# A gated mix of a long convolution and linear attention: the layout of three DRAM round trips, and the issue order of the second half

## The chip, the cores and the metric

The kernel runs on one core of a Trainium2 chip. The time is the device time of one execution in microseconds (us). Before the change it is 265.62 us, the median of 3 runs (265.59 to 265.95).

## The reference

The input `A_u` has 2048 rows of 512 columns (bf16). Two branches read it, and a gate per row mixes them:

```python
g = sigmoid((x * gate_w).sum(-1))
a = irfft(rfft(u) * rfft(K)) + u * Dskip      # K[d, l] = Re sum_n C exp(dt A l) dt B, 128 n per column d
phi_q = [softmax(q @ w_phi), softmax(-q @ w_phi)]    # 32 heads of 16; phi_k alike
o = phi_q (phi_k^T v) / (phi_q sum(phi_k) + 1e-6)
out = g * a + (1 - g) * (o @ wo)
```

The convolution runs along the 2048 rows, for each of the 512 columns.

## The kernel before, in words

**Steps and their order.** The kernel is a list of 1058 steps (class `Plan`). A step has an engine, a function that issues its instructions, and the steps on which it depends. Three strings written out by hand fix the rest: `ORDER` the order in which the steps are issued, `SIDES` which of two engines a movable step gets (mostly ACT or DVE), and `RINGS` which PSUM buffers it uses. Each engine executes its instructions in the order of issue. DMAs are issued on SP, except for a few stores of the result on ACT; a DMA that must wait for data holds up everything behind it on the engine that issues it. Steps that only mark the transfer or the arrival of a DMA issue nothing.

**Tables.** The convolution kernel K is made for 32 columns at a time, in sixteen tables 0 to 15. For each, DVE multiplies C and D tables into A (L1100, L1105, in half of the tables also a sum L1110), ACT makes E by exp and cs by sin, DVE makes a second E (L1053) and R from E and cs (L1117, L1121), and PE multiplies A and R (kps, L183). A has one buffer, R two. The result is cast to SBUF (KD), transformed by PE (psA, L190) and cast again (XA).

**Transforms.** The 512 columns are four groups of 128. Groups 0 to 2 are transformed whole, from four tables each; group 3 in three parts: tables 12 and 13 (64 columns), table 14 (32) and table 15 (32). A transform goes: PE psB (L196), cast XK, DVE multiplies by the spectrum XUX of the input, loaded from DRAM (t, L1231 or L1234), PE psz (L1263), cast Zr. Then the data must change partitions (the *turn*): Zr is stored in the DRAM scratch Zd (L1276) and loaded back as ZT (L1285). PE makes the output psy from ZT (L1341), and DVE scales it by the gate into xT (L1363, L1366). Table 15 goes without the turn: its psz (L1297) is cast to Z and used in SBUF (L1354, L1369). A group of 128 columns has four stores Zd and two loads ZT, one of each half of the partitions.

**Attention.** Blocks of 512 rows: pq, exp (Eq), the denominators zs, and a chain of small steps on ACT and DVE (z steps, L878 to L886) that gives the normaliser apm. It is stored to DRAM (apd, L899) and loaded back, each row copied to 16 partitions (ax, L906); DVE multiplies Eq by it (L913). Then follow the products ops (L932), their casts oT, and the output products bps (L946). Three blocks come early; the fourth, the *late* block, runs beside the last tables. Its bps are cast into xT (L981, L983), and stored by L995.

**Stores.** The result is stored by L1380 for groups 1 to 3 (group 1 together with group 0; of groups 0 to 2 the late block's rows are left to L995). Group 3 is stored in two sets: columns 384 to 447 when tables 12 and 13 are through, columns 448 to 511 at the end.

Of the kernel before, what the change touches and what calls it, by code (L numbers as in the profile page):

```python
# [70 lines left out]
class Plan:  # L71

    DIGITS = "0123456789abcdefghijklmnopqrstuvwxyzABCDEFGHIJKLMNOPQRSTUVWXYZ-_"
    ORDER = ("040B0H0K0d0y0C0D0L0s0I070J0M0P0g000S110j0N08010z0T0m0Q0e2R0a0p0q0r0_0W2T100U0O0V14120Y2U2x0A2S050k130Z2y2V2X2Z0R190v0t0u"
             "0b0c0w2_0l0E0X2W1516172L1a061b2Y022-30311y33340n030f0-"
             "0h1e1f0i1w2J18321c0F0o2B2K2M1n1z1H1g1A1o2D2C1d1p1I091x1E1J351Q1R2F1B0x1C2E0G2H1q36372G2I2P382N2Q391F3b2O3c4C1S3a4J4L4K4M"
             "3d3e4Q4R3f4U1Y3g4N1r4O1h4V3h1L4Y4-"
             "4P3i4Z4_3j4W4S53542z57504T3k4X1Z515b5d58521s1D593l5c3n5i5e55565j3m5a1G3o5q5f5g5s5r5t3p3r3q1T5m5n5u3s5v5h5o5k5w5x5B1P4D4E"
             "3w2v5l5p4F5y5F5C3y1U5H3x5G5I5J5z5A1V5D5E3t3z5U3D5K5V5M5N3A3R3E2w3F5W5L1O5_3G5O5Q5X5Y5Z3B3C1W605R5S1N3K3M1K3S1M5-"
             "5P3L634G642A615T653N673T6869626a666m6n6o3U6p3V3W3X3Y6b6c6q6d6r6s1t3Z3H3-1X3_3O1i1j41401_4221431-"  # L80
             "1k1l204445466e272923222b282d4748243P491m2a4a2c2e4b4g2f4c2g4d252h2o4e4h4i4n1u4j3u3v2j4p2i2l2k2m2q2p6i262s4q4o1v4k2n4u2r2t"
             "6f4v4w6j4r3I2u4x4y4z6g4l8l3J4A8p8m6t6u6k6v8q3Q4f4s6x6h8k8o6l8n8r8s6y6z6w6A6C4m4t4B8C6G8t6I6K8w8x8y8u6B6H6J4H8D8v6L6M6N7d"
             "8z8A8E4I8B7e7f8I7g8F6F9e8Q8G8H9b6O6P8R7h7j7i6Q6R8J9f7M7N8S6S6T6U6Vaeaf7O8W8X8K7k9g8L8T8U8Z8-"
             "938M8N7l6D8_7m8V7n6W6X6Y8O8P8Y7P94an7o7pao7q6_70717r90917Qa47S9295ag7R6Z7s6-"
             "72aha8a9966Ea7akaca5ai73aa75979998ajap7677a69aalatamab74ad7TaBaC7t797u7v7U78au7y7z7V7w7x9caq9naras7AavaH7W9d9h9o9paw7X9v"
             "aY9waK7Y7ZaDaL9q9raZ7a9x9y9zaIc57B7-aM9kc69D9EaQaEbX9L7Cb_aF7D9M7_9Ac07EaRaG9iaxaz80ay9B818285bYaA7Ga-"
             "7IaJ86879j9Fc19s7Jb-"
             "9l9m9Na_7bc7aNaOaPc3cbb2b37HbZc283aS9C7FaT849G9H9I9t89aUaWaV8baX7cccc8c99O9u9P9Q9R888cb87Kb9b0c4caceb19J8abacfcgbg8dck9K"
             "8ecl8f8gbbbh8hbcbibob4cP9Sbpbqcd9T8ichci7L8jcBcCcjcsdYcYctcucycDczdZd-cQcR9Ucmd_cHcvcw9W9Xcnbj9VbwbkblbxcocIbre0eLcp9Ze1"
             "e2b5b6eMbse3eUeVcxb7bye4cqbtbu9Ybdbe9-"  # L90
             "9_cAcrcSbme5cZdOdScEbfcFcGcTcUe6a0a1bve7dTdRdWeNa2e8cJcKe9bzbAedeecLeRcNcOa3eSeaebeOcMc_ePbBd0ecd1d7cVd8d9cWeCdfcXeWdPdU"
             "d2daefege-e_eQd3dbdQdgeTdVd4dndodXdhdcg1g2dieDeEdjeXbKfAbCbnbDbEbFeYfBeZf0f1bGc-dpbLddg7dqbHd5f2drbMf3f4f5bNfGbIbJbOezdk"
             "eAfDdsfEeBeIf6f7feffdldtbPdebQdBfCfHehdueifFejdmf8fgeJd6ekdvfIfJdyf9fafhfbg4fifKg5g6dwfjdzfkfcdxdCdEfLdAdFfMg3g8dGg9dHfN"
             "fleFelfdfmfpdDdLgagbgcgddIeGemeKfqeHfOfPfQfRgeenepfneofreqeresgfggghgifSfTfUfofsbRgjbSgkdJftetglfVfYfZgmgngobUbVgqfufWdM"
             "dNbWgpf-fvfxfygreufwevewexbTeydKfzfXf_g0gvgwgsgtgugx")
# [103 lines left out]
def prepare(P, nc, g, evict, psum):  # L199

    fc, act, persist, at = g.fc, g.act, g.persist, g.at
    F = Bag()
# [35 lines left out]
    S("ifc", lambda: nc.scalar.copy(out=F.fi[:], in_=F.ii[:]), r="ic0", w="ic1")  # L238
# [33 lines left out]
    def sine(out, v, kv, w, turn=False):  # L272
        S("tgs", lambda: act(out=out(), in_=(low(v()) if not turn else low(v()).rearrange("p (h t) -> p t h", h=2)), func=ACT.Sin, scale=TURN), r="act " + kv, w=w)
# [786 lines left out]
def plan_conv(P, nc, g, psum, r):  # L1060
# [130 lines left out]
    def transform(XA, ready, Q, off, nd, far, Ls, last, co=0, free=True, split=False):  # L1191
# [9 lines left out]
        if far:  # L1201
            F.Zd = g.dram.tile([32, 4, 32, nd], BF16, name=f"Zd{Q}_{off}")
# [423 lines left out]
```

## Time and profile before

| | |
|---|---|
| median of the runs | 265.62 us |
| the profiled execution | 266.07 us |
| its span, first to last instruction | 264.3 us |
| mean granted TensorE clock | 0.932 of full speed |
| busy: DVE, ACT, PE | 232.5, 221.5, 207.2 us |
| DMA packets | 63323, of which 40496 are under 512 B |
| last multiply of DVE ends | 257.69 us |

The profile is of one execution. A line L1231 is that line of the kernel; casts stand under the two lines of a helper (L149 on ACT, L151 on DVE), so they are told apart by their tiles. SPq and ACTq are the DMA issues of SP and ACT. The chain of work that ended last is followed back from the end, at each step to what released it; its pieces have a start, a length and a name.

### The profile page before, as it was taken

How to read it: one execution, taken by the hardware profiler on the slowest of the kernel's cores; microseconds unless marked ns; L12 is line 12 of the kernel's file. 1: busy time of each engine (PE TensorE's matmuls, PEld its weight loads, DVE VectorE, ACT ScalarE, POOL GpSimd, SP SyncE). 2: the span in 40 equal slices, each digit the busy share in tenths (PEclk: the TensorE clock that was granted, in tenths of full speed). 3: DMA queues.
4: the chain of work that ended last, by engine and by line, in shares of the span. 5: the costliest groups of instructions: out<-in, count | busy, mean ns of one | idle time of the engine just before them, and what ended most of it. 6: DMA issues, size and time to landing. Idle time of an engine off the chain costs nothing.

```text
span 264.3 us, 10050 instructions
## 1 busy us (share of the span) xinstructions
PE 207.2 (78%) x4491; PEld 143.7 (54%) x4512; DVE 232.5 (88%) x315; ACT 221.5 (84%) x305; POOL 8.2 (3%) x21
## 2 busy tenths in 40 slices
PE   0766999999864879889776768999997598999750
PEld 0655655656633533456555247665775176965540
DVE  6699989889799999999999997999997998997630
ACT  6999998998899999899999898999998597755100
POOL 4700000000000000000000000000000000000000
PEclk9999999999976599999998688999999799999985
DMA  6995000454501892204160655159554589999775
GB/s 201 189 219 171 0 4 2 122 145 138 154 8 36 245 266 97 82 20 153 56 195 9 208 195 167 42 162 180 142 172 147 172 203 234 188 189 162 156 110 96
DMA packets 63323, 35.93 MB, mean 136 GB/s; under 512 B 40496, under 2 KB 57776, under 8 KB 63280
## 3 DMA queue, kind: packets, MB, share of 16 engines
q1 hardware_dynamic: 61424, 34.76, 53.2%
q8 instruction: 35, 0.57, 1.0%
q10 hardware_dynamic: 1856, 0.52, 1.0%
q14 instruction: 8, 0.07, 0.1%
HBM read 22.17 MB, written 13.11 MB: 133 GB/s over the span
## 4 chain that ended last, share of the span: by engine, by line
DVE 35%; PE 34%; DMA 8%; issue 7%; ACT 7%; SPq 6%; DVEq 0%; ACTq 0%
PE pk L709 5%; PE vp L757 4%; DVE Eq L913 3%; DVE A L1105 3%; DVE A L1100 3%; DMA ZT<-Zd 3%; DVE R L1117 3%; DVE R L1121 3%; SPq L1492 3%; DMA ax<-apd 2%; PE kps L183 2%; DVE E L1053 2%; PE psz L1263 2%; PE kvp L774 2%; DMA apd<-apm 2%
## 5 line engine op out<-in xcount | busy, mean ns | idle before, releaser
L68 ACT ACTIVATE cs<-args 128x1024 bf16<-128x1024 f32 x32 | 30.7, 1067 | 0.7 <-PE args L1023 0.7
L183 PEld LDWEIGHTS <-A 128*32 128x32 bf16 x1536 | 26.5, 160 | 6.1 <-issue 2.3
L183 PE MATMUL kps<-R,A 128*32 128x64 bf16 x1536 | 28.2, 229 | 1.9 <-DVE R L1121 1.2
L1263 PE MATMUL psz<-t,TI 128*128 128x512 bf16 x51 | 17.4, 446 | 5.0 <-DVE t L1231 3.2
L1100 DVE TENSOR_TENSOR A<-Ctab,Dtab 128x2048 bf16<-128x2048 bf16 x16 | 19.5, 1216 | 1.6 <-PE kps L183 1.6
L149 ACT CAST Zr<-psz 128x1024 bf16<-128x1024 f32 x15 | 15.2, 1021 | 5.8 <-PE psz L1263 4.3
L1121 DVE TENSOR_TENSOR R<-E,cs 128x2048 bf16<-128x2048 bf16 x16 | 19.4, 1215 | 0.1
L1105 DVE TENSOR_TENSOR A<-Ctab,Dtab 128x2048 bf16<-128x2048 bf16 x16 | 19.4, 1216 | 0.0
L1117 DVE TENSOR_TENSOR R<-E,cs 128x2048 bf16<-128x2048 bf16 x16 | 19.4, 1215 | 0.0
L68 ACT ACTIVATE Ek<-pk 128x512 bf16<-128x512 f32 x32 | 16.7, 599 | 1.9 <-PE pk L709 1.7
L68 ACT ACTIVATE Eq<-pq 128x512 bf16<-128x512 f32 (+1 forms) x28 | 16.6, 685 | 0.8 <-PE pq L843 0.7
L1231 DVE TENSOR_TENSOR t<-XUX,XK 128x2048 bf16<-128x2048 bf16 x14 | 16.7, 1216 | 0.4 <-ACT XK L149 0.4
L68 ACT ACTIVATE E<-args 128x1024 bf16<-128x1024 f32 x16 | 16.4, 1035 | 0.5 <-DVE R L1121 0.5
L757 PE MATMUL vp<-WW,xT 128*128 128x512 bf16 x59 | 16.2, 406 | 0.7 <-issue 0.6
L149 ACT CAST XA<-psA 128x1024 bf16<-128x1024 f32 (+1 forms) x15 | 14.6, 1002 | 2.4 <-PE psA L190 2.4
L843 PE MATMUL pq<-xT,Wqp 128*128 128x512 bf16 x64 | 15.5, 380 | 0.3 <-ACT xT L149 0.3
L616 PE MATMUL psB<-XAu,TB 64*128 64x128 bf16 x256 | 11.6, 250 | 5.1 <-ACT xst L149 3.4
L149 ACT CAST XK<-psB 128x1024 bf16<-128x1024 f32 (+1 forms) x14 | 13.6, 989 | 2.2 <-DVE XK L151 1.3
L709 PE MATMUL pk<-WW,xT 128*128 128x512 bf16 x58 | 15.0, 380 | 0.4 <-issue 0.2
L616 PEld LDWEIGHTS <-TB 64*128 64x128 bf16 x256 | 9.6, 110 | 8.9 <-issue 8.8
L190 PE MATMUL psA<-W,KD 128*64 128x128 bf16 x256 | 10.0, 223 | 5.1 <-ACT cs L68 2.9
L65 ACT ACT_TABLE_LOAD x10 | 12.8, 1283 | 0.2
(211 smaller groups left out, 503.8 us busy)
## 6 DMA issues: line engine op xcount, KB each, us to landing
XUX<-XUd SPq DMA_DIRECT2D x32, 256.0 KB
XUd<-xst SPq DMA_DIRECT2D x8, 512.0 KB
ax<-apd SPq DMA_DIRECT2D x16, 256.0 KB
Zd<-Zr SPq DMA_DIRECT2D x15, 256.0 KB
ZT<-Zd SPq DMA_DIRECT2D x6, 512.0 KB
UD<-in_A_u_dram SPq DMA_DIRECT2D x16, 128.0 KB
XUd<-xst SPq DMA_DIRECT2D x8, 256.0 KB
wqk<-in_B_wqkv_dram SPq DMA_DIRECT2D x1, 1024.0 KB
```

What stands on the lines that cost most here:

```text
L68: return self.nc.scalar.activation(**kw)
L149: self.nc.scalar.copy(out=o, in_=i)
L183: nc.tensor.matmul(kps[32 * dj:32 * dj + 32, g4, e, :], lhsT=A[:, ka, :, :, d].rearrange("p a b -> p (a b)"), rhs=R[:, kr, d, :], start=(i ...
L616: nc.tensor.matmul(box.ps[:, c2, sl, :], lhsT=fc.TB[rows, b0:b0 + 2].rearrange("p a b -> p (a b)"), rhs=X.t[rows, k, r0 + sl].rearrange("p ...
L709: nc.tensor.matmul(box.ps[:], lhsT=xT[:, st, kt, :], rhs=g.WW[:, kt, :], start=(kt == 0), stop=(kt == 3))
L757: nc.tensor.matmul(box.ps[:], lhsT=xT[:, st, kt, :], rhs=g.WW[:, 4 + kt, :], start=(kt == 0), stop=(kt == 3))
L1100: nc.vector.tensor_tensor(out=c.A[:, 0:2].rearrange("p o a b c -> p (o a) b c"), in0=g.C[U // 8][:, 0:2, :, d0 % 256:d0 % 256 + 32].rearra ...
L1105: nc.vector.tensor_tensor(out=c.A[:, 2:4].rearrange("p o a b c -> p (o a) b c"), in0=g.C[U // 8][:, 1:3, :, d0 % 256:d0 % 256 + 32].rearra ...
L1117: nc.vector.tensor_tensor(out=c.R[:, :, :, 32:64], in0=t.E[:, 1].unsqueeze(1).to_broadcast([128, 2, 32, 32]), in1=t.cs[:], op=ALU.mult)
L1121: nc.vector.tensor_tensor(out=c.R[:, :, :, 0:32], in0=t.E[:, 0].unsqueeze(1).to_broadcast([128, 2, 32, 32]), in1=t.cs[:, ::-1, :, ::-1], o ...
L1231: nc.vector.tensor_tensor(out=box.t, in0=Ls[r0 // ns].X[:], in1=box.XK[:].unsqueeze(1).to_broadcast([128, 2, 1024]), op=ALU.mult)
L1263: nc.tensor.matmul(box.ps[:, hb, :], lhsT=fc.TI[:, k].rearrange("p t h a -> p (t h a)"), rhs=box.t[:, k, 512 * hb:512 * hb + 512], start=( ...
```

## The change

Six edits. The two tables of numbers are left out of the diff, but for a word.

1. The turn's scratch Zd is laid out by the row that loads it: row r holds all t and x of its columns in one run (8 KB for 128 columns), and rows are padded by 1024 elements. A store of Zr now writes pieces of 128 columns (256 bytes; 128 and 64 bytes in group 3), where it wrote 2 KB runs; a load ZT reads one run for each partition, where it read 32 pieces. Each load of half the partitions is issued as two of 32 partitions. The table TI gets its axes in the matching order.
2. The normaliser is stored twice (two DMAs apd), so that the load sees 16 rows of DRAM copied 8 times each, where it saw 8 rows copied 16 times.
3. Columns 384 to 511 are stored as one set at the end: four DMAs of 128 columns, where there were eight of 64 columns at two points. That leaves 1052 steps.
4. The very first cast (column indices to float) goes from ACT to DVE.
5. The steps from number 605 on are issued in another order. Up to DVE's multiply L913 of the third block, near 170 us in the trace, each engine has the rows that it had, apart from edits 2 and 4.
6. Of the movable steps behind that point some change engines. From DVE to ACT: an XK of group 1, an XA of group 2, the XK of table 14, half of XA, XK and Z of table 15, one cast of bps. From ACT to DVE: net one oT, the Zr of table 14, two scalings of bps (L983).

```diff
 class Plan:
-    ORDER = ("040B0H0K0d0y0C0D0L0s0I070J0M0P0g000S110j0N08010z0T0m0Q0e2R0a0p0q0r0_0W2T100U0O0V14120Y2U2x0A2S050k130Z2y2V2X2Z0R190v0t0u"
+    ORDER = ("0405060B0C0D0H0K0d0e0f0y0z0A0L0s0t0u0I0708090J0M0P0g0h0i000S110j0k0l0N0102030T0m0n0o0Q2R0a0b0c0p0q0r0_0W2T100U0O0V14120Y"
...
-    S("ifc", lambda: nc.scalar.copy(out=F.fi[:], in_=F.ii[:]), r="ic0", w="ic1")
+    V("ifc", lambda: nc.vector.tensor_copy(out=F.fi[:], in_=F.ii[:]), r="ic0", w="ic1")
...
         def aw():
-            nc.sync.dma_start(out=g.apd[b].rearrange("i h m c -> (i h m) c"), in_=Q.apm[:].rearrange("p s t -> p (s t)"))
+            for u in range(2):
+                nc.sync.dma_start(out=g.apd[b, :, :, u].rearrange("i h m c -> (i h) m c"), in_=Q.apm[:].rearrange("p s t -> p (s t)"))
...
-                                  in_=g.apd[b, i].rearrange("h m c -> h (m c)").unsqueeze(1).to_broadcast([8, 16, 1024]))
+                                  in_=g.apd[b, i].rearrange("h u m c -> (h u) (m c)").unsqueeze(1).to_broadcast([16, 8, 1024]))
...
-        lo = 64 if last else off
+        lo = 0 if last else off
...
-            F.Zd = g.dram.tile([32, 4, 32, nd], BF16, name=f"Zd{Q}_{off}")
+            F.Zd = g.dram.tile([32, 128 * nd + 1024], BF16, name=f"Zd{Q}_{off}")[:, 0:128 * nd].rearrange("r (x t d) -> r x t d", x=4, d=nd)
...
-                nc.sync.dma_start(out=F.Zd[:, :, r0:r0 + ns, :].rearrange("t x r d -> (t x) r d"), in_=box.Z[:])
+                nc.sync.dma_start(out=F.Zd[r0:r0 + ns].rearrange("r x t d -> (x t) r d"), in_=box.Z[:])
...
-            nc.sync.dma_start(out=F.Z[64 * th:64 * th + 64], in_=F.Zd[:, 2 * th:2 * th + 2].rearrange("t x r d -> (x r) t d"))
+            for x in (2 * th, 2 * th + 1):
+                nc.sync.dma_start(out=F.Z[32 * x:32 * x + 32].rearrange("p t d -> p (t d)"), in_=F.Zd[:, x].rearrange("r t d -> r (t d)"))
...
-            if end and Q != 0 and (nd > 32 or last):
+            if end and Q != 0 and (Q < 3 or last):
```

Three places of the order. **First, DVE where the orders part**, behind the multiply L913 of the third block (the last row that is alike; L909 after). t is the multiply by the spectrum, A and R make the tables, oT and XK are casts. Before:

```order
L913 TENSOR_TENSOR Eq<-Eq,ax 128x2048
L151 CAST oT_2103<-ops 128x512
L151 CAST XK<-psB 128x1024
L1110 TENSOR_TENSOR A<-A 128x2048
L1231 TENSOR_TENSOR t<-XUX,XK 128x2048
L1053 TENSOR_TENSOR E<-E,Gtab 128x1024
L1117 TENSOR_TENSOR R<-E,cs 128x64x32
L1121 TENSOR_TENSOR R<-E,cs 128x64x32
L1231 TENSOR_TENSOR t<-XUX,XK 128x2048 x2
L1100 TENSOR_TENSOR A<-Ctab_75,Dtab 128x2048
L1105 TENSOR_TENSOR A<-Ctab_75,Dtab 128x2048
```

and now:

```order
L909 TENSOR_TENSOR Eq<-Eq,ax 128x2048
L146 CAST oT_2103<-ops 128x512
L1106 TENSOR_TENSOR A<-A 128x2048
L146 CAST oT_2104<-ops 128x512
L1227 TENSOR_TENSOR t<-XUX,XK 128x2048
L1096 TENSOR_TENSOR A<-Ctab_75,Dtab 128x2048
L1101 TENSOR_TENSOR A<-Ctab_75,Dtab 128x2048
L1227 TENSOR_TENSOR t<-XUX,XK 128x2048
L1049 TENSOR_TENSOR E<-E,Gtab 128x1024
L1113 TENSOR_TENSOR R<-E,cs 128x64x32
L1117 TENSOR_TENSOR R<-E,cs 128x64x32
```

The XK cast is gone from DVE, an oT cast has come, and A of table 9 stands ahead of its R, right behind the first t.

**Second, SP around the late block's normaliser.** XUX loads the spectrum, apd and ax are the normaliser's way out and back, Zd1 and ZT the scratch of group 1, Zd2 that of group 2. Before:

```order
L1184 DMA XUX_4242<-XUd_117 128x2x512 x2
L899 DMA apd_118<-apm_4103 128x256
L906 DMA ax_4452<-apd_118 128x1x1024 x4
L1276 DMA Zd1_0_120<-Zr_4460 128x1024
L1184 DMA XUX_4531<-XUd_117 128x2x512 x2
L1186 DMA XUX_4537<-XUd_117 128x1024 x2
L1276 DMA Zd2_0_121<-Zr_4571 128x1024
L1276 DMA Zd2_0_121<-Zr_4573 128x1024
L1285 DMA ZT_4786<-Zd1_0_120 64x32x128 x2
```

and now:

```order
L895 DMA apd_118<-apm_4113 32x4x256 x2
L1180 DMA XUX_4307<-XUd_117 128x2x512 x2
L902 DMA ax_4502<-apd_118 128x1x1024 x4
L1272 DMA Zd1_0_120<-Zr_4495 128x8x128
L1272 DMA Zd1_0_120<-Zr_4515 128x8x128
L1180 DMA XUX_4699<-XUd_117 128x2x512 x2
L1282 DMA ZT_4763<-Zd1_0_120 32x4096 x2
L1272 DMA Zd2_0_121<-Zr_4707 128x8x128
L1282 DMA ZT_4763<-Zd1_0_120 32x4096 x2
```

The XUX load that stood ahead of apd now stands behind it, and the first load ZT of group 1 is issued ahead of the stores of group 2 instead of behind two of them.

**Third, ACT at the end of the program**, from the last KD cast on. The stores of L1380 (L1377) are those of groups 0 and 1 and then of group 3; L991 stores columns of the late block. Before:

```order
L149 CAST KD_5440<-kps_5350 128x256 x2
L149 CAST XA_4898<-psA_5443 128x32x16
L149 CAST xT_68<-bps_5421 128x2x128
L149 CAST Zr_5471<-psz_5466 128x1024
L981 ACTIVATE xT_68<-bps_5421,gT_66 128x384
L981 ACTIVATE xT_68<-bps_5475,gT_66 128x384
L149 CAST XK_5526<-psB_5493 128x512
L149 CAST Z_5601<-psz_5602 128x64x8
L1380 DMA out_0_dram<-xT_68 32x12x256 x2
L1380 DMA out_0_dram<-xT_68 512x1x64 x2
```

and now:

```order
L144 CAST KD_5430<-kps_5351 128x256 x2
L144 CAST oT3_5033<-ops_5421 128x1024
L144 CAST XA_4887<-psA_5440 128x32x16 x2
L144 CAST xT_68<-bps_5468 128x2x128
L144 CAST XK_5518<-psB_5485 128x512 x2
L144 CAST xT_68<-bps_5525 128x2x128
L1377 DMA out_0_dram<-xT_68 32x12x256 x2
L144 CAST Z_5541<-psz_5542 128x64x8 x2
L991 DMA out_0_dram<-xT_68 32x4x384 x2
L1377 DMA out_0_dram<-xT_68 512x1x128 x2
```

Both halves of XA, XK and Z of table 15 are now ACT's, an oT cast of the late block has come in front, and the store of groups 0 and 1 stands ahead of the Z casts. On PE, psB of table 14 stood directly ahead of kps of table 15; now a pya and a psy stand between them. Between that kps and the last psB PE had bps, psA, psz, bps; now it has ops, psA, psz, bps, and the other bps comes behind that psB. Before the last psz PE had psy of tables 12 and 13; now that psy stands between its two halves.

69 lines of the change are left out of this document (32 added, 37 removed).

## The prediction

> **What bounds the kernel now.** I read the busy shares first, then a table by stretches, then DVE's waits, then the chain that ended last, then the timeline of the two DMA queues at the end.
>
> ```profile
> PE 207.2 (78%) x4491; PEld 143.7 (54%) x4512; DVE 232.5 (88%) x315; ACT 221.5 (84%) x305; POOL 8.2 (3%) x21
> 170.00:190.00 20.00, 18.87 (x391) 13.43 (x391) 19.97 (x22) 19.43 (x25) 0.00 (x0) 1.00 0.76 147
> 200.00:212.00 12.00, 7.47 (x115) 4.44 (x116) 10.29 (x10) 8.59 (x11) 0.00 (x0) 0.86 0.57 180
> 245.00:258.00 13.00, 7.84 (x429) 6.06 (x427) 6.32 (x10) 1.75 (x3) 0.00 (x0) 0.90 0.72 132
> 258.00:264.30 6.30, 0.00 (x0) 0.00 (x0) 0.00 (x0) 0.00 (x0) 0.00 (x0) 0.50 0.58 96
> ```
>
> The rows by stretches give, after the length, the busy time of PE, weight load, DVE, ACT and POOL, then the granted clock, the DMA share and GB/s. They show three regimes. Up to about 237 us DVE is the bound: 19.97 of 20 us at 170 to 190, and ACT close behind. From 245 us on no engine is full: it is one chain of small steps. In the last 6.3 us no engine works; only stores run.
>
> ```profile
> DVE Eq L913 <- DMA ax<-apd: 1.7, 1, 1.7
> DVE A L1100 <- PE kps L183: 1.6, 1, 1.6
> DVE xT L1366 <- PE psy L1341: 1.1, 1, 1.1
> DVE t L1231 <- ACT XK L149: 0.4, 1, 0.4
> ```
>
> These are DVE's waits from 150 to 237 us: 4.8 us in all, of which the 1.6 lies before the point where the orders part (169.85 us). 3.2 us is what a better order can give back while DVE is the bound. What makes two of them stands in the chain:
>
> ```profile
> 193.80 4.54 DMA apd<-apm
> 200.34 5.88 DMA ax<-apd
> 212.47 7.92 DMA ZT<-Zd
> ```
>
> The late block's normaliser takes 4.54 us to reach DRAM and 5.88 us to come back; the second group's turned scratch takes 7.92 us.
>
> **The change, part by part.**
>
> *Casts taken from DVE.* Before table 15 is built, DVE loses one XK and one XA cast and gets one oT cast more.
>
> ```profile
> 169.85 0.68 DVE L151 CAST oT<-ops 128x512 bf16<-128x512 f32 x1
> 170.45 1.21 DVE L151 CAST XK<-psB 128x1024 bf16<-128x1024 f32 x1
> 171.58 1.21 DVE L1110 TENSOR_TENSOR A<-A 128x2048 bf16<-128x2048 bf16 x1
> 201.04 1.22 DVE L151 CAST XA<-psA 128x1024 bf16<-128x1024 f32 x1
> 202.18 1.22 DVE L1105 TENSOR_TENSOR A<-Ctab,Dtab 128x2048 bf16<-128x2048 bf16 x1
> ...
> L149 ACT CAST XK<-psB 128x1024 bf16<-128x1024 f32 x13 | 13.1, 1020 | 0.9 <-PE psB L196 0.9
> ```
>
> From start to start these cost 0.60, 1.13 and 1.14 us, so DVE does 1.13 + 1.14 - 0.60 = **1.7 us** less. ACT takes them over (1.0 us each). That is nothing where ACT has room (8.59 of 12 us at 200 to 212), and its whole price where it has none (19.43 of 20): then DVE waits for the cast instead, and the 1.7 shrinks to nothing.
>
> *Normaliser as 16 rows, and its place in SP's queue.* While the four ax loads run, the DMA share is about half, though work is queued; the XUX loads reach more:
>
> ```profile
> 147.00:148.50 1.50, 1.50 (x5) 0.48 (x4) 1.50 (x3) 1.07 (x2) 0.00 (x0) 0.50 0.82 264
> 201.00:205.00 4.00, 2.33 (x42) 1.98 (x37) 2.39 (x3) 3.63 (x5) 0.00 (x0) 1.00 0.56 193
> 205.10 1.22 DVE L913 TENSOR_TENSOR Eq<-Eq,ax 128x2048 bf16<-128x2048 bf16 x1 [1.71 <-DMA ax<-apd]
> ```
>
> At 264 instead of 193 GB/s the 1 MB comes in 4.0 instead of 5.4 us. Also, the XUX load ahead of apd in SP's queue now goes behind it. Together some 2 to 3 us off a path on which DVE waits 1.71: the wait goes. The second apd store adds one issue on SP, inside this. [...]
>
> *The turn's scratch.* The 256-byte pieces move from the load, which comes after the last cast, to the stores, of which only the last one counts. The pieces of a whole group stay 4096 in number.
>
> ```profile
> 214.00:218.00 4.00, 3.51 (x47) 2.80 (x46) 3.97 (x5) 3.97 (x5) 0.00 (x0) 1.00 0.87 155
> 228.50:232.00 3.50, 3.45 (x82) 2.71 (x81) 3.50 (x4) 2.52 (x3) 0.00 (x0) 1.00 1.35 186
> ```
>
> Here the old loads run: 155 to 186 GB/s, so half a group (524 KB) takes 2.8 to 3.4 us. The last store (262 KB in pieces) should then take about 1.5 us instead of 1.0 at 264 GB/s, and the half load 2.0 instead of 3.1: about 0.6 us less on the path to the first psy. The DVE wait of this kind is the 1.1 at xT: there SP issued the load of the second group behind two stores of the third, and now it issues it ahead of them (rows of SP above). So that wait goes too, and I count it with the waits below. The price of a store in pieces is not in this trace: from 96 GB/s (the row of the last 6.3 us, 128-byte and 768-byte pieces) to 264, it takes 2.7 to 1.0 us. I take 1.5, which lies with the loads in pieces, the nearest rows. Padding changes addresses only; nothing.
>
> *Waits in the new order.* Stepping DVE's rows by the durations above from 169.85 us, I find four waits: 0.4 for the second oT cast, 0.5 where A of table 9 stands directly behind the multiply t and needs kps of table 8, 1.3 where the z steps come before zs has passed PE, and 0.6 for XK of the third group. That is 2.8 instead of 3.2: **-0.4**. The bounds are -3.2 (no wait) and +3.2 (twice as many).
>
> *kps of table 15.* It stood behind a psB; now that psB comes earlier, and its XK cast is ACT's.
>
> ```profile
> 186.44 0.97 PE psz L1263 x4
> 228.34 1.75 PE ops L932 x16
> 235.77 1.23 DVE L1121 TENSOR_TENSOR R<-E,cs 128x2048 bf16<-128x2048 bf16 x1
> 237.03 0.90 PE psB L196 x32
> 237.92 1.14 PE kps L183 x62
> 239.44 0.59 PE bps L946 x2
> 241.45 0.59 PE psA L190 x16
> 243.42 1.02 PE bps L946 x4
> 249.47 2.32 PE psz L1297 x114
> ```
>
> DVE ends R at 237.0, kps starts at 237.92: **-0.9**, nothing at worst (if scratch for psy, now ahead of it, is late).
>
> *The last chain.* From the end of kps (239.4) to the last psz (249.47) there are 10.0 us. Two output products bps, of about 2.1 us each, stand on PE ahead of the last psB, and XK then waits on DVE behind their casts. Now one of them stands there, with an ops (1.75) instead of the other, half of it under the KD cast; XK goes to ACT. I take **-1.0**. The bounds: -2.5, a bps and the DVE queue both gone, and +2.1, below. Zr of table 14 goes to DVE (1.2) in a stretch with 6.32 of 13 us busy: nothing.
>
> *Columns 384 to 511 as one set.* Four stores of 64 KB at an early point and their issues go, and the last four carry 128 KB each.
>
> ```profile
> 251.25 7.84 SPq L1380 DMA_DIRECT2D out_dram<-xT  x4
> 252.54 2.10 ACTq L1380 DMA_DIRECT2D out_dram<-xT  x2
> 257.00 0.69 DVE L1366 TENSOR_TENSOR xT<-psy,gT 128x512 bf16<-128x512 f32 x1 [0.74 <-PE psy L1341]
> 259.13 1.17 SPq L995 DMA_DIRECT2D out_dram<-xT  x2
> 260.40 1.27 SPq L1380 DMA_DIRECT2D out_dram<-xT  x2
> 260.00:262.00 2.00, 0.00 (x0) 0.00 (x0) 0.00 (x0) 0.00 (x0) 0.00 (x0) 0.50 0.99 175
> ```
>
> DVE ends at 257.69, but SP is still issuing the early set until 259.1, so the last two issues start at 260.40 and end at 261.67; the span ends 2.6 us later. From DVE's end that is 6.6 us. Now SP and ACT issue two each at once: 1.3, then 2.6, and twice the bytes cost about 1.3 us more at 175 GB/s (the last 256 KB): 5.2, so **-1.4**. The bounds are -2.6 (longer pieces cost nothing) and 0.
>
> *The first cast on DVE* takes a table load off ACT. The start waits for the loads that SP issues, until 18.87 us:
>
> ```profile
> 14.87 4.00 DMA UD<-in_A_u_dram
> 18.88 1.04 ACT xT L149
> ```
>
> So nothing; at best 0.5.
>
> **Sum.** -1.7 - 0.4 - 0.9 - 1.0 - 1.4 = **-5.4 us**. The profiled execution took 266.07 us (span 264.3 and 1.8 around it), which gives 260.7; the median of the runs is 265.62, 0.45 lower, so **260.2 us**.
>
> **The rivals.**
>
> A, *a store stands ahead of the Z casts.* On ACT the store of columns 0 to 255 now comes before both Z casts; before, it came after. Its two issues held ACT for 2.10 us from 252.54 on, with nothing behind them that anyone waited for. For it: the Z casts are on the last chain. Against: the first psz half and the psy now between the halves run meanwhile. If nothing hides it, the last chain's -1.0 becomes +1.1, so 262.3; with the stores at the end no shorter either, 263.7.
>
> B, *DVE waits for its A buffer (slower).* A has one buffer, and DVE builds A of tables 9 to 15 each time close behind the kps that reads it; the trace shows such a wait once, 1.6 us. Queued behind A on DVE are R and t, and all of PE's next kps. Five such waits of 1.6 are 8.0 us; with the other terms -1.7, -0.9, -1.0 and -1.4 the sum is +3.0 (268.6). It decides from 5.0 us of waits more than today. For it: in the new rows A follows t directly at table 9. Against: by my count PE has mostly finished kps by then.
>
> C, *small pieces make the scratch store slow.* The last scratch store is 4096 pieces of 64 bytes. At 186 GB/s of 256-byte pieces there are 727 pieces per us: 5.6 us. R ends at 234.9 by my sum; kps 1.4, ops and psA 2.3, psz 1.0 and Zr 1.2 put the store at 240.8. With 2.6 us to land, 3 for the load, 1.4 for psy and the last xT and 5.2 at the end, a store of 11.3 us (362 pieces per us, half the rate) ends the span where it ends now; below that it decides, and at a third (16.9 us) the time is 271.7 by the profiled execution's count, slower by 5.6. [...] The old stores of 128-byte pieces, 175 GB/s with larger ones among them, do not show a loss of that size.
>
> D, *16 rows spread no better.* DVE's 1.7 stays: 261.9. It lies inside the range.
>
> **How the numbers follow.** A difference within 0.2% (0.5 us) can't be told from none. Forecast, D with it: 0.68, from 256.8 (waits gone and the chain shorter) to 263.2. Still better than that: 0.04. A: 0.13, up to 264.6 with a little waiting on DVE. B: 0.10. C: 0.03. About the same as before, because the gains meet a part of B: 0.02. The range 256.8 to 264.6 holds the forecast and A, 0.81. Faster: 0.68 + 0.04 + 0.13 = 0.85; same 0.02; slower 0.10 + 0.03 = 0.13.
>
> **What would show it.** Right: no wait of Eq for ax; ax loads at a DMA share near 0.8; R of table 15 ended by about 235 us; after the last xT, stores for about 5 us, issued by SP and ACT side by side. Wrong: waits of A for kps over 3 us (B), ACT's Z casts late behind a store (A), psy waiting for ZT by several us (C), or ACT over 99% busy at 170 to 200 with DVE waiting for XK.

## The result and the profile after

| | before | changed |
|---|---|---|
| median of 20 runs each | 265.03 us (263.23 to 266.75) | 262.36 us (260.65 to 265.88) |
| ratio, 95% interval | 1 | 0.9895 [0.9867, 0.9924] |
| two later comparisons | 1 | 0.9945 [0.9891, 0.9998] and 0.9930 [0.9889, 0.9971] |
| profiled execution, span | 266.07, 264.3 us | 265.88, 264.1 us |

The forecast was 260.2 us, 5.4 below the median shown. Measured is 2.7 less than before (1.5 and 1.9 by the ratios of the later comparisons): faster, inside the range, about half the size. All three profiles of the changed kernel are of executions 3.5 to 4.2 us above the median of their group (265.88, 266.77, 266.55 against 262.36, 263.27, 262.32) and that of before is 1.0 above its own, so they show where time stands and not how much is won. Experiment 2 has a profile of nearly the same kernel 0.3 us above its median, and its sum is there.

First the busy shares of the changed kernel, its table by stretches (length, busy time of PE, weight load, DVE, ACT and POOL, granted clock, DMA share, GB/s), its DVE waits from the fork to the end of table 15, and the transfers on its chain there. The *fork* is the start of DVE's multiply Eq of the third block, the last row of DVE that is alike; the end of table 15 is that of DVE's last operation for it.

```profile
PE 210.0 (80%) x4512; PEld 145.4 (55%) x4512; DVE 231.2 (88%) x313; ACT 221.7 (84%) x306; POOL 8.3 (3%) x21
```
```profile
170.00:190.00 20.00, 18.79 (x392) 13.39 (x389) 19.80 (x20) 19.50 (x24) 0.00 (x0) 1.00 0.64 160
200.00:212.00 12.00, 9.81 (x251) 6.77 (x244) 11.76 (x12) 12.00 (x14) 0.00 (x0) 1.00 0.79 201
245.00:258.00 13.00, 9.21 (x428) 6.39 (x424) 5.65 (x10) 2.82 (x6) 0.00 (x0) 0.91 0.71 134
```
```profile
DVE t L1227 <- ACT XK L144: 0.4, 1, 0.4
DVE Eq L909 <- DMA ax<-apd: 0.2, 1, 0.2
```
```profile
195.44 3.42 DMA apd<-apm
199.59 4.83 DMA ax<-apd
226.68 6.57 DMA ZT<-Zd
```

At 200 to 212 DVE is now full (11.76 of 12, before 10.29) and so is ACT (12.00, before 8.59). From the fork DVE waits 0.6 us instead of 3.2; the normaliser goes out in 3.42 us and comes back in 4.83 (before 4.54 and 5.88). The ZT load of group 2 (columns 256 to 383) takes 6.57 (its second DMA; 6.94 from the first DMA's issue). What it does stands in PE's and DVE's rows at the end of table 15 (a bracket is the idle time ahead, and what ended it), with the clock beside them in stretches of 2 us. The first fence has the fork, before and now, and kps of table 15 before:

```profile
168.71 1.21 DVE L913 TENSOR_TENSOR Eq<-Eq,ax 128x2048 bf16<-128x2048 bf16 x1
170.60 1.22 DVE L909 TENSOR_TENSOR Eq<-Eq,ax 128x2048 bf16<-128x2048 bf16 x1
237.85 1.21 PE L183 MATMUL kps<-R,A 128*32 128x64 bf16 x64
```

```profile
230.13 0.64 PE L185 MATMUL psA<-W,KD 128*64 128x128 bf16 x16
233.30 0.63 PE L1338 MATMUL psy<-ZT,TJ 64*32 64x128 bf16 x32 [2.53 <-DMA ZT<-Zd]
234.73 0.99 PE L191 MATMUL psB<-XA,TB 128*128 128x32 bf16 x32
238.90 1.22 PE L178 MATMUL kps<-R,A 128*32 128x64 bf16 x64
```
```profile
233.65 1.21 DVE L1106 TENSOR_TENSOR A<-A 128x2048 bf16<-128x2048 bf16 x1
239.03 0.69 DVE L1360 TENSOR_TENSOR xT<-psy,gT 128x512 bf16<-128x512 f32 x1 [4.17 <-PE psy L1338]
```
```profile
232.00:234.00 2.00, 0.70 (x33) 0.56 (x34) 2.00 (x3) 0.00 (x0) 0.00 (x0) 1.00 0.94 148
234.00:236.00 2.00, 2.00 (x41) 1.56 (x40) 0.86 (x1) 1.03 (x2) 0.00 (x0) 0.78 0.42 137
236.00:238.00 2.00, 2.00 (x22) 2.00 (x19) 0.00 (x0) 0.90 (x1) 0.00 (x0) 0.50 0.92 212
```

DVE ends table 15 at 234.86. PE, though, has stood 2.53 us for ZT, and behind that psy wait psz, psB, pya and a second psy; the clock falls to 0.50 while it makes them up. kps starts at 238.90, 4.04 us after its table (before 0.85, by PE's row above; the 0.92 of the prediction is from the chain). The wait and the clock account for it: the clock stood at 0.50 for 3.41 us (235.12 to 238.53) with PE busy throughout, an estimated 1.7 us of work at full clock, and 2.53 + 1.7 is 4.2. DVE, bound until then, waits 4.17 us. Counted from the fork, SP issues that load after 55.7 us (57.2 and 57.5 in the two repeats of experiment 1), where it was 57.65 before, and the end of table 15 comes after 64.3 (65.2, 64.6), where it was 68.3. DVE's tables came 3.1 to 4.0 us earlier, the load of group 2 only 0.1 to 1.9.

The end: PE's rows of the last chain, and DVE's last operation with the last stores.

```profile
252.45 0.28 PE L1294 MATMUL psz<-TI,t 128*32 128x64 bf16 x4 [1.47 <-issue]
256.45 0.21 PE L1351 MATMUL psy<-Z,TJ 64*32 64x16 bf16 x8 [1.67 <-issue]
```
```profile
257.90 0.69 DVE L1363 TENSOR_TENSOR xT<-psy,gT 128x512 bf16<-128x512 f32 x1 [0.74 <-PE psy L1338]
258.66 1.33 SPq L1377 DMA_DIRECT2D out_dram<-xT  x2
258.67 1.63 ACTq L1377 DMA_DIRECT2D out_dram<-xT  x2
```

SP and ACT issue the last stores side by side right at DVE's end (258.59), and the span ends 5.5 us later instead of 6.6. PE stops twice without a releaser, 3.14 us together (before once in its last chain, 1.02 us).

Put together, the profile after against that of before: up to the fork (Eq of the third block, 168.71 and 170.60) +1.9, from there to the end of table 15's last DVE operation 68.3 and 64.3, so -4.0, to the start of kps +3.2, from kps to DVE's end 19.84 and 19.69, so -0.15, and the stores -1.1: -0.2 in all.

### The profile page after: what moved, and what is told of

It reads as the page before. It is cut to its first block, busy times and chain, and to the rows that moved or that the text cites. A ratio compares the mean times of both kernels' runs of the same rounds, so it can differ in the third digit from the quotient of the medians.

```text
span 264.1 us, 10087 instructions
## 1 busy us (share of the span) xinstructions
PE 210.0 (80%) x4512; PEld 145.4 (55%) x4512; DVE 231.2 (88%) x313; ACT 221.7 (84%) x306; POOL 8.3 (3%) x21
## 4 chain that ended last, share of the span: by engine, by line
PE 38%; DVE 23%; ACT 21%; DMA 9%; issue 6%; SPq 1%; POOL 0%; DVEq 0%; ACTq 0%; POOLq 0%
PE pk L704 6%; PE vp L752 5%; DMA ZT<-Zd 5%; ACT cs L68 4%; PE psz L1259 3%; DVE R L1113 3%; PE kps L178 3%; ACT L65 2%; PE psA L586 2%; DMA ax<-apd 2%; DVE R L1117 2%; DVE A L1096 2%; PE kvp L769 2%; PE psB L611 2%; PE psA L185 2%
## 5 line engine op out<-in xcount | busy, mean ns | idle before, releaser
L144 ACT CAST Zr<-psz 128x1024 bf16<-128x1024 f32 x14 | 14.7, 1053 | 4.5 <-issue 3.1
L144 ACT CAST XK<-psB 128x1024 bf16<-128x1024 f32 (+1 forms) x17 | 16.7, 1003 | 2.1 <-PE psB L191 2.0
L1259 PE MATMUL psz<-t,TI 128*128 128x512 bf16 x60 | 16.4, 397 | 2.1 <-ACT XK L144 0.8
L752 PE MATMUL vp<-WW,xT 128*128 128x512 bf16 x64 | 17.5, 414 | 0.0
L144 ACT CAST XA<-psA 128x1024 bf16<-128x1024 f32 (+1 forms) x17 | 16.2, 997 | 0.2 <-PE psA L185 0.2
L704 PE MATMUL pk<-WW,xT 128*128 128x512 bf16 x64 | 16.2, 393 | 0.0
L185 PE MATMUL psA<-W,KD 128*64 128x128 bf16 x256 | 10.8, 233 | 4.0 <-ACT cs L68 2.1
L191 PE MATMUL psB<-XA,TB 128*128 128x128 bf16 (+2 forms) x192 | 11.3, 209 | 3.0 <-ACT XK L144 0.9
```

Source lines behind the costliest of these rows:

```text
L144: self.nc.scalar.copy(out=o, in_=i)
L704: nc.tensor.matmul(box.ps[:], lhsT=xT[:, st, kt, :], rhs=g.WW[:, kt, :], start=(kt == 0), stop=(kt == 3))
L752: nc.tensor.matmul(box.ps[:], lhsT=xT[:, st, kt, :], rhs=g.WW[:, 4 + kt, :], start=(kt == 0), stop=(kt == 3))
L1259: nc.tensor.matmul(box.ps[:, hb, :], lhsT=fc.TI[:, k].rearrange("p h a t -> p (h a t)"), rhs=box.t[:, k, 512 * hb:512 * hb + 512], start=( ...
```

## The experiments

Each was timed beside the kernel before, and the ratio is to that. The expectations count the groups of columns from zero: their second group is group 2, their third is group 3. Code fences here are cut: "..." stands for lines left out, and a fence with an engine's name gives that engine's order in words.

**1. The changed kernel again, twice.** No edit.

> The changed kernel again, for a second profile of it. In the first profile the time gained between the point where the orders part and the last DVE operation of table 15 was 4.0 us (168.71 to 237.0 before, 170.60 to 234.87 after), and three losses stood against it: 1.9 us at the fork, about 2 us at kps of table 15 (forecast -0.9, measured +1.05), and 1.0 in the last chain, which came out no shorter. Theory 1: all three belong to the change; the second profile shows them again (xT of the first block near 19.4 instead of 18.9 us, kps of table 15 about 4 us behind the end of A of table 15, a psy waiting over 2 us for ZT). Theory 2: the loss at the start belongs to that one execution (the granted clock fell to 0.50 at 28 us); then the second profile has the fork within 0.7 us of 168.7, and the time is that much shorter. Time near 262.

> The changed kernel a third time, because both profiles of it so far are of executions 3.5 us above its median. Theory 1, the long wait of psy for ZT (2.5 and 2.7 us) and the low clock behind it (0.50 to 0.83 at 230 to 240 us, with table 15's kps 4 to 5.6 us behind the end of its A) belong to every execution: a profile near the median shows both again, and is shorter elsewhere. Theory 2, they belong to the long executions: ZT comes earlier, PE waits under 1.5 us, the clock stays at 1.00 at 230 to 240 and kps starts within 2 us of the end of its A.

0.9945 and 0.9930 (above). Fork at 169.19 and 171.23; from there to the end of table 15 65.2 and 64.6 us; psy waits 2.69 and 1.92 for ZT, the clock falls to 0.50 behind it both times, kps starts 5.6 and 4.0 us after its table. So the wait and the low clock stand in all three profiles of this kernel, while the loss ahead of the fork varies from 0.5 to 2.5 us. As none of these executions was near the median, whether the timed ones have the wait too is left to experiment 2.

**2. The first cast on ACT again.**

```diff
-    V("ifc", lambda: nc.vector.tensor_copy(out=F.fi[:], in_=F.ii[:]), r="ic0", w="ic1")
+    S("ifc", lambda: nc.scalar.copy(out=F.fi[:], in_=F.ii[:]), r="ic0", w="ic1")
```

> One part undone: the cast of the first indices stands on ACT again, where it cost a table load. Theory 1, the cast on DVE costs time: it starts only when POOL's iota is done and pushes DVE's and ACT's first steps back by 0.4 to 0.5 us; here the first xT copy on ACT returns to 18.9 us, and the whole is 0.5 us shorter than the changed kernel. Theory 2, the start waits for loads anyway, as the forecast had it: the first xT copy stays where the changed kernel has it, and so does the time (within 0.3 us).

0.9936 [0.9878, 0.9994]; the time does not resolve half a microsecond. The trace does: rows of the changed kernel (the cast, POOL's iota beside it, the first xT), then the first xT here.

```profile
1.81 1.32 DVE L233 CAST if<-ii 128x8 f32<-128x8 int32 x1
```
```profile
1.11 2.00 POOL L41 IOTA tgc<- 128x2048 f32 x1
```
```profile
19.41 1.95 ACT L144 COPY xT<-xps 128x1024 bf16<-128x1024 bf16 x2
```
```profile
18.99 1.95 ACT L144 COPY xT<-xps 128x1024 bf16<-128x1024 bf16 x2
```

The cast of 8 columns ends on DVE with POOL's iota (3.13 and 3.11 us), where ACT's was done at 2.22. In the five profiles with the cast on ACT the first xT starts at 18.87 to 19.08, in the nine with it on DVE at 19.25 to 20.06. The move costs about 0.5 us at the start: theory 1 there; that the whole gets 0.5 us shorter is not shown.

This kernel differs from the changed one in that cast alone, and its profiled execution is 0.3 us above the median (264.35, 264.06). So its rows answer what experiment 1 left open:

```profile
231.69 0.63 PE L1338 MATMUL psy<-ZT,TJ 64*32 64x128 bf16 x32 [1.86 <-DMA ZT<-Zd]
237.19 1.21 PE L178 MATMUL kps<-R,A 128*32 128x64 bf16 x64
```

Here, near the median, psy waits too, the clock stands at 0.50 for 3.41 us behind it, and kps starts 3.27 us after its table. The fork is at 168.71, as before the change; from there to the end of table 15 are 65.2 us (before 68.3), from kps to DVE's end 19.9 (19.8), and the stores take 5.5 (6.6). That is -3.1 + 2.4 + 0.0 - 1.1 = -1.7 us, and the ratio says -1.7.

**3. The XUX load behind the ZT loads.**

```diff
 SP
-    store Zd   load XUX (group 3)   load ZT (group 2)   store Zd
+    store Zd   load ZT (group 2)   load XUX (group 3)   store Zd
```

> The XUX load that SP issues directly ahead of the second group's two ZT loads (223.46 us in the first profile) goes behind them. Theory 1, table 15's kps is late because PE stands on the psy that waits for ZT, and ZT shares the DMA engines with XUX: ZT lands 1.5 to 2 us earlier, psy's wait of 2.5 us shrinks to about 1, kps of table 15 starts 2 to 2.5 us behind the end of its A instead of 4, and the time falls by 1 to 2 us. Theory 2, ZT is slow by its own packets (8 KB each at about 0.55 us): it lands at most 0.5 us earlier and the time stays.

```profile
230.59 0.63 PE L1338 MATMUL psy<-ZT,TJ 64*32 64x128 bf16 x32 [1.80 <-DMA ZT<-Zd]
```

0.9984 [0.9942, 1.0026]. The wait is 1.80 us and kps starts 3.25 after its table: somewhat better than the changed kernel's three profiles (1.92 to 2.69; 4.0 to 5.6), the clock falls all the same (to 0.50 at 232 to 234), and the time is no better. From SP's first issue to psy it is 6.1 us, inside the 5.6 to 7.0 of the changed kernel. Sharing is not the main cause of the late ZT; theory 2 is nearer.

**4. psy behind kps.** Numbers are tables; psy, with its halves, is that of group 2.

```diff
 PE
-    psA14  psy(1st half)  psz13  psB14  pya, psy(2nd half)  kps15  ops  psA15  psz14  bps  psB15  bps
+    psA14  psz13  psB14  kps15  psy(1st half)  ops  psA15  psz14  pya, psy(2nd half)  psB15  bps  bps
```

> On PE the second group's first psy goes behind kps of table 15, and its pya and second psy behind psA of table 15 and the psz of the third group; DVE's and ACT's steps that read them move along, and the output product of the last blocks stands behind the last psB. Theory 1, the psy that waits for ZT is what holds kps of table 15 back: kps starts within 0.6 us of the end of its A instead of 4.0 us behind it, the last psB comes 2 to 4 us earlier, and the time falls by 2 to 4 us against the changed kernel, to about 259. Theory 2, the end is set by the last chain and the stores, not by kps: kps comes early as well, but the last xT and the time stay within 0.7 us.

```profile
232.17 1.23 PE L178 MATMUL kps<-R,A 128*32 128x64 bf16 x64 [2.06 <-DVE A L1106]
240.26 0.96 PE L191 MATMUL psB<-XA,TB 128*128 128x32 bf16 x32
245.71 1.18 PE L1294 MATMUL psz<-TI,t 128*32 128x64 bf16 x64 [0.15 <-DVE t L1230]
```

kps starts 0.05 us after its table, and yet the ratio is 1.0049 [1.0001, 1.0097]: slower than the changed kernel, whose first repeat ran beside it (0.9945). Theory 1's second half, the gain in time, falls. kps to the last psB takes 8.1 us (changed 5.7), psB to psz 5.45 (3.06): what stood ahead of kps now stands behind it, and here the XK casts queued behind a reader of bps.

**5. The end in a third and a fourth order.** ops ahead of kps, psA15 behind psy, XK casts and t ahead of the readers of bps; in the second one also psz14 and its store early (pszn is table 15's psz, psy64 the psy of tables 12 and 13), the other stores ahead of the last ZT loads, and the first cast on ACT.

```diff
 PE (third)
+    psB14  ops  kps15  psy(1st half)  psA15  pya, psy(2nd half)  psB15  psz14  bps  bps  pszn  psy64
 PE (fourth)
+    psB14  ops  kps15  psy(1st half)  psA15  psz14  pya, psy(2nd half)  psB15  bps  bps  pszn  psy64
```

> The end of the changed kernel in a third order, after the run in which psy went behind kps came out 2 to 3 us slower than the changed kernel although kps of table 15 started right at the end of its A (232.17 us): there the last XK casts and t stood behind a copy and a multiply of the output product bps on ACT and DVE (last psB to last psz 5.45 instead of 3.06 us), and ops and pya stood ahead of psA and psB (kps to last psB 8.1 instead of 5.7). Here ops stands ahead of kps, psA right behind kps and psy, the XK casts and both t ahead of every reader of bps, and both bps ahead of the last psz. Theory 1, the late ZT costs the changed kernel its gain at kps, and the loss of the earlier run was its own order: the last psB ends 4 to 6 us earlier than in the changed kernel and the time falls to 257 to 260. Theory 2, the end is held by PE waiting for its own instruction stream (two stalls of 1.2 to 1.8 us each, without a releaser, in each run of the new order) and by the ZT loads one after another: kps and psB come early, and the time stays within 1 us of the changed kernel.

> The third order of the end with what held it removed: the psz of the third group directly behind psA of table 15, its cast on ACT and its scratch store ahead of the ZT loads in SP's queue (there the last ZT load waited for 4096 pieces of 64 bytes that ended at 246.65 us), the stores of the columns 0 to 383 ahead of the last ZT loads (there SP still issued them 3 us after DVE's end), and the first cast on ACT again. Theory 1, these two held the earlier run: the last ZT load is issued at about 244.5 instead of 247.8, the last stores right at DVE's end, the tail falls from 7.5 to 5.5 us and the span by 3 to 4 us (to about 258). Theory 2, PE's stops without a releaser and the chain of casts decide: DVE's end moves by less than 0.5 us and only the tail's 2 us are won.

In the third, from its chain, kps, the last psB, the first half of the last psz, and the stop ahead of the last 4 matmuls of its second half; then DVE's last operation and SP's stores around it:

```profile
231.17 1.21 PE kps L178 x53
236.11 0.90 PE psB L191 x32
242.23 1.08 PE psz L1294 x60
245.53 2.24 issue
247.77 0.30 PE psz L1294 x4
```
```profile
253.44 0.69 DVE L1363 TENSOR_TENSOR xT<-psy,gT 128x512 bf16<-128x512 f32 x1 [0.96 <-PE psy L1338]
```
```profile
250.71 4.51 SPq L1377 DMA_DIRECT2D out_dram<-xT  x4
256.62 1.85 SPq L1377 DMA_DIRECT2D out_dram<-xT  x2
```

1.0014 [0.9981, 1.0047] and 1.0010 [0.9956, 1.0065]: no faster than before. The third refutes theory 1, and it is even slower than theory 2 allows, which had the time of the changed kernel within 1 us. Its profile is of an execution 2.3 us below the median, with the fork at 167.25, so it is counted from the fork. kps and the last psB come 4.4 and 5.2 us earlier than in the profile after, the first half of the last psz 2.2, DVE's end (254.13) 1.1, and the span ends 0.9 later. It leaks away at a PE stop of 2.24 us, at the last ZT load, which waited for 4096 pieces of 64 bytes (moved from 242.51 to 246.65), and at stores still in SP's queue. In the fourth the tail is back at 5.8 us, but the last ZT loads start only at 252.40, behind stores that had not finished, and DVE ends at 255.43, which neither theory had. From the end of table 15 to DVE's end it is 23.0 and 23.3 us, in the changed kernel 23.7, 25.1 and 23.5, before 20.7.

PE's load in that stretch grew with it (from the end of table 15 to DVE's end, before, then changed, then third order):

```profile
237.00:257.69 20.69, 15.35 (x565) 10.71 (x564) 11.78 (x17) 5.34 (x10) 0.00 (x0) 0.95 0.81 149
```
```profile
234.86:258.59 23.73, 19.35 (x629) 14.28 (x625) 10.49 (x16) 8.04 (x14) 0.00 (x0) 0.87 0.71 147
```
```profile
231.12:254.13 23.01, 17.45 (x620) 12.31 (x620) 10.59 (x15) 5.21 (x12) 0.00 (x0) 0.90 0.64 133
```

After DVE's tables, PE is busy 15.35 us before and 19.35 after (17.45 in the third order). Each piece weighed by the clock granted at that moment, that is an estimated 14.7, 17.0 and 16.4 us at full clock: about 2 us more work, and the rest is the low clock. DVE got ahead; PE's part of group 2 did not. That this load is what holds the end is read from these rows: no run takes work off PE alone.

**6. The three layouts in the old order.** Padded scratch, 16 rows and one store set, steps of before but for the early stores that go.

```diff
-        lo = 64 if last else off
+        lo = 0 if last else off
...
-            F.Zd = g.dram.tile([32, 4, 32, nd], BF16, name=f"Zd{Q}_{off}")
+            F.Zd = g.dram.tile([32, 128 * nd + 1024], BF16, name=f"Zd{Q}_{off}")[:, 0:128 * nd].rearrange("r (x t d) -> r x t d", x=4, d=nd)
...
```

> The three layouts (padded scratch, 16 rows, one store set) in the order of before, first cast on ACT as before. Theory 1, what the change gained comes from layouts: DVE's wait of 1.71 us for ax goes, the end from the last xT to the end of the span falls from 6.6 to 5.5 us, kps of table 15 still follows its table by 0.9 us: 2.5 us faster than before, as fast as the changed kernel or faster. Theory 2, it comes from the order (DVE's casts on ACT, 1.7 us): the fork to the last operation of table 15 stays above 67 us (68.3 before, 63.7 to 65.2 in the runs of the new order), and the time is 1 us or less below before.

```profile
247.68 6.04 SPq L1282 DMA_DIRECT2D ZT<-Zd  x4
```
```profile
255.91 0.40 PE L1338 MATMUL psy<-ZT,TJ 64*32 64x32 bf16 x32 [2.81 <-DMA ZT<-Zd]
```

1.0031 [0.9990, 1.0072]. The time refutes theory 1, and theory 2's stretch is missed as well: the fork to the end of table 15 is 66.7 us, 1.6 less than before (DVE waits 0.8 for ax), and kps follows in 0.25. But the end gives it back: SP takes 6.04 us to issue the last ZT load, now four transfers instead of two, and in the chain it stands behind a store that had not landed; psy waits 2.81. The order of before was made for fewer transfers (the list counts the doubled ones as one here), so the run does not show what the layouts would give in an order fitted to them.

**7. The new order with the old scratch and 8 rows.** The scratch as in experiment 9, and:

```diff
-                                  in_=g.apd[b, i].rearrange("h u m c -> (h u) (m c)").unsqueeze(1).to_broadcast([16, 8, 1024]))
+                                  in_=g.apd[b, i].rearrange("h m c -> h (m c)").unsqueeze(1).to_broadcast([8, 16, 1024]))
...
```

> The new order with one store set, but the scratch and the normaliser laid out as before (8 rows, 256-byte pieces in the load). Theory 1, the layouts make the load of ZT and ax faster: here ax is waited for again by 1 to 2 us, ZT lands later still and PE's wait for it grows from 2.5 to 3 or 4 us; the time is 1 to 3 us above the changed kernel, at or above before. Theory 2, the layouts change nothing and the place of the loads in SP's queue does: the fork to the last operation of table 15 is 63.7 to 65.2 us again and the time that of the changed kernel.

The normaliser's load here, then in the changed kernel, and Eq here:

```profile
201.00:205.00 4.00, 3.08 (x46) 1.68 (x44) 4.00 (x4) 4.00 (x6) 0.00 (x0) 1.00 0.61 226
```
```profile
200.50:204.50 4.00, 3.46 (x58) 1.87 (x52) 3.77 (x4) 4.00 (x6) 0.00 (x0) 1.00 1.00 263
```
```profile
203.93 1.22 DVE L908 TENSOR_TENSOR Eq<-Eq,ax 128x2048 bf16<-128x2048 bf16 x1
```

1.0016 [0.9974, 1.0058]. With 16 rows the DMA share is 1.00, with 8 rows 0.61. But Eq does not wait with 8 rows either: in the new order the load's place in SP's queue is enough. psy's wait for ZT is 3.3 us, and kps starts 4.7 us after its table. Theory 1 has the time, theory 2 the stretch from the fork (64.4 us). This execution is 0.6 us below its median, so it shows why the new order gains nothing here: the 3.9 us that it wins from the fork to the end of table 15 are lost again by the start of kps.

**8. 16 rows alone, in the kernel before.**

```diff
-        g.apd = dram.tile([4, 4, 8, 4, 256], BF16, name="apd")
+        g.apd = dram.tile([4, 4, 8, 2, 4, 256], BF16, name="apd")
...
```

> The kernel before with one part of the change alone, the normaliser stored and read as 16 rows. Theory 1, more rows spread the load over more DMA engines: the four ax loads of the last block run at a DMA share near 0.8 instead of 0.56, DVE's wait of 1.71 us for ax falls below 0.7, the time by 1 to 1.5 us. Theory 2, the share of 0.56 came from waiting for the store and SP's queue: the share and the wait stay within 0.3 us.

0.9942 [0.9902, 0.9983]: about 1.5 us, and Eq's wait of 1.71 us is gone (DMA share 0.83 at 201 to 205). The fork to the end of table 15 falls from 68.3 to 65.9 us. Theory 1.

**9. The old scratch alone, in the changed kernel.**

```diff
-                nc.sync.dma_start(out=F.Zd[r0:r0 + ns].rearrange("r x t d -> (x t) r d"), in_=box.Z[:])
+                nc.sync.dma_start(out=F.Zd[:, :, r0:r0 + ns, :].rearrange("t x r d -> (t x) r d"), in_=box.Z[:])
...
```

> The changed kernel with the turn's scratch alone laid out as before (256-byte pieces in the load, none under 128 bytes in the stores); the 16 rows, the one store set, the first cast on DVE and the new order stay. So far the 16 rows alone, in the old order, gave 0.9942 of the time before, all three layouts in the old order 1.0031, the new order with the scratch and the normaliser both as before 1.0016, the changed kernel 0.9895, 0.9945 and 0.9930. Theory 1, the new scratch layout is worth its part in the new order too: without it ZT lands later, the wait of psy is above 3 us as in the run with both old layouts (3.3), and the ratio is 0.998 or more. Theory 2, only the 16 rows matter of the layouts, and the scratch in pieces of 64 bytes gives back at the end what it wins before (the last store took 3 to 4 us): the ratio is 0.994 or less, and the last ZT load is issued earlier relative to the cast before it.

0.9885 [0.9847, 0.9924], of six runs: as good as the changed kernel. Its profile has a psy wait of 2.67 us, like the changed kernel's. The new scratch is worth nothing that these runs show, and with experiment 7 the 16 rows carry the gain of the layouts: theory 2. From its first issue to landing the half load of group 2 takes 7.03 us (7.29 in experiment 7; 6.94, 6.82 and 5.53 in the changed kernel, whose half goes as two DMAs). The part on an earlier last load is not borne out: it is issued 6.3 us after the cast of Zr of table 14, in the changed kernel 6.2.

**10. 124 small matmuls at PE's start.**

```diff
...
+                for _ in range(124):
+                    nc.tensor.matmul(g.lead[0:32, 0, 0:16], lhsT=g.ident[:, 0:32], rhs=g.ident[:, 0:16], start=True, stop=True)
...
```

> The changed kernel with 124 very small matmuls more at the start of PE's program, where PE waits for wqk; nothing reads their result. In the last chain of the changed kernel PE stops twice with nothing to wait for, once after 60 of the 64 matmuls of the second half of the last psz and once, 128 matmuls later, after 56 of the 64 of the second last psy; each time a 16 KB transfer of the instruction queue has landed 1.3 to 1.5 us before PE goes on. Theory 1, PE has run out of loaded instructions, and a transfer carries 128 matmuls with their weight loads: 124 more move both stops by exactly 4 matmuls (64 of 64, and 60 of 64), the first then lies in the wait for the cast of Z and costs up to 0.7 us less. Theory 2, the stops come from the data, the PSUM or the stores that run beside: they stay at 60 and 56.

```profile
249.03 1.13 PE L1299 MATMUL psz<-TI,t 128*32 128x64 bf16 x63
251.99 0.22 PE L1299 MATMUL psz<-TI,t 128*32 128x64 bf16 x1 [1.84 <-issue]
253.80 0.62 PE L1356 MATMUL psy<-Z,TJ 64*32 64x16 bf16 x59
256.00 0.20 PE L1356 MATMUL psy<-Z,TJ 64*32 64x16 bf16 x5 [1.57 <-issue]
```

0.9921 [0.9874, 0.9969], as the changed kernel. Both stops moved, from 60 to 63 and from 56 to 59, by 3 instead of 4 (the added lines may have brought an instruction or two more). They follow the count of instructions, not the data, as theory 1 had it; that PE had run out of loaded instructions is not shown by it. They did not get shorter. Here psy waited only 0.81 us for ZT, the clock stayed at 1.00, and kps came 1.6 us after its table: nearly the same kernel can run without the long wait, and this execution, 2.7 us above its median, was no fast one for it. Its fork was at 171.58.

## Why the forecast was half right

- *DVE's casts, -1.7, and waits, -0.4*: right in direction, too small. The fork to the end of table 15 gave 4.0, 3.1 and 3.7 us. The casts were sized well: DVE's busy time there falls from 64.9 to 63.4 us. The waits were not: I counted 2.8 us of them in the new order, and the profile after shows 0.6; all of DVE's idle time there falls from 3.4 to 0.9.
- *Eq's wait for ax*: fell to 0.2 (0.9 and 1.2 in the repeats, 1.1 in experiment 2), so it did not go as forecast, at a DMA share of 1.00 where I expected 0.8. I gave rows and queue place the credit together. Each takes the wait away alone (experiments 7 and 8); why some of it is left with both is open.
- *kps of table 15, -0.9, "nothing at worst"*: **the step that failed.** It measured +3.2 in the profile after and +2.4 in the one near the median (experiment 2). I named the condition, "if scratch for psy, now ahead of it, is late", and then put the bound at nothing, because I took DVE's table for the limit and PE for free. PE's wait for ZT and the low clock after it are the price (2.53 and an estimated 1.7 us). Experiments 4 and 5 add that the delay alone does not decide: with kps on time the time was not shorter.
- *The last chain, -1.0*: measured -0.15 from kps to DVE's end (19.84 to 19.69 us). PE's stops are 3.14 us instead of 1.02; that it would be shorter without this difference of 2.1 is argued, as no run took the stops away.
- *Stores as one set, -1.4*: -1.1. SP and ACT issue two each at DVE's end, as forecast. Part of the difference is a slip of the sum: 256 KB more at 175 GB/s are 1.5 us, not 1.3.
- *The first cast, nothing*: costs about 0.5 us at the start (experiment 2). I had looked at SP's loads only; ACT's and DVE's first steps were on the path as well.
- *The turn's scratch, about 0.6 less to the first psy*: not settled. From SP's first issue to that psy it is 6.99, 6.86 and 5.58 us in the changed kernel, 7.07 and 7.33 with the old scratch (experiments 9 and 7), so 0.1 to 1.8 less. Undoing it costs no time (experiment 9).
- *The rivals*: A did not happen (ACT's store 247.80 to 248.72, the Z cast at 248.87 waited for psz, not for it). B did not: no wait of A for kps. C's sign came, psy waiting 2.5 us for ZT, but in group 2, whose stores are in 256-byte pieces; the 64-byte store took 3.1 us, not 11. D's premise is refuted by the share of 1.00.

The right direction thus rests on two terms that were mostly right, DVE's and the stores', with 16 rows the one layout that shows in the times. DVE's and the stores' terms do not carry it alone: experiment 7 has both and gains nothing. Open are why 8 rows in the new order cost 1.3% (experiments 7 and 9, on the same chip) though no wait for ax is left in the profile, and what the timed executions of the changed kernel do better than its three profiled ones. Part of it may lie ahead of the fork, which stands anywhere from 167.1 to 171.6 us in the 14 profiles. That the late kps cost the missing half is not shown by a run either: with kps on time (experiments 4 and 5) the time was no shorter.

## What to carry to other kernels

When work is taken off the engine that bounds a stage, sum what the next engine still has to do in that stage, from that point to the end: here DVE ended its tables 3 to 4 us earlier, and PE was then busy for 4.0 us more, of which about 2 were work and the rest a low clock. And a profile far from the median of its kernel is counted from a common row, not by its absolute times. A condition that a forecast names ("if this load is late") deserves a price worked out from that load's own row: group 2's ZT load was issued at 226.36 us before the change, and its psy now stood ahead of kps.

## What the runs showed of the hardware

- The granted clock after a wait of PE at the end of table 15: in eight profiles PE waited there in one piece for 1.80 to 3.3 us, and each time the clock then stood at 0.50 for a while (profile after: a wait of 2.53 us, then 0.50 from 235.12 to 238.53). Behind the waits of 0.81 us (experiment 10), 1.2 and 1.18 us (third and fourth order) it stayed at 1.00. The length of one wait does not decide: 1.88 us ahead of the last psz left the clock at 1.00 before the change, and 1.9 and 1.88 us ahead of the same psz were followed by 0.50 in experiments 6 and 8. What does decide is not shown. Two stretches of the kernel before around that wait, then the one ahead of the fall in the changed kernel (PE busy 2.32, 2.52 and 1.82 us of 3.41):

```profile
245.26:248.67 3.41, 2.32 (x102) 1.62 (x99) 2.21 (x4) 1.15 (x2) 0.00 (x0) 1.00 0.84 207
248.67:252.09 3.42, 2.52 (x130) 2.34 (x131) 2.16 (x4) 0.02 (x1) 0.00 (x0) 1.00 0.60 85
```
```profile
231.71:235.12 3.41, 1.82 (x52) 1.25 (x53) 3.15 (x3) 0.29 (x2) 0.00 (x0) 1.00 0.67 105
```

- In its last chain PE stopped without a releaser: twice in the profile after (1.47 and 1.67 us), once before (1.02 us). The two lie 128 matmuls apart, and each ended 1.5 us after a transfer of 16 KB in the instruction queue had landed (250.98 and 252.45, 254.94 and 256.45). With 124 matmuls more at PE's start both stood 3 matmuls further on in the same rows (experiment 10). That PE had run out of loaded instructions is the author's reading; no run shows what it waited for.

- A DVE cast of 8 columns took 1.32 us beside POOL's iota and ended with it (3.13 and 3.11 us); before, on ACT, it took 0.20.
